# Moving columns read in runs of 16 from two halves of a row, and weight buffers on four places modulo 256 bytes

## The chip, the cores and the metric

The kernel runs on one core of a Trainium2 chip. The metric is the device time of one execution in microseconds (us). Before the change it is 827.43 us, the median of three runs (826.84 to 827.73).

The engines are named as the profile names them: PE (TensorE, matmuls), PEld (its weight loads, which run beside matmuls), DVE (VectorE), ACT (ScalarE), POOL (GpSimd) and SP (the queue that issues the transfers). SBUF is the working memory, 128 partitions wide; PSUM is where matmuls accumulate.

## The reference

A sigmoid attention is followed by a channel mix. All of it is float32; the inputs are scaled by factors that are left out here.

```python
# q, k, v: (8, 12, 448, 64)
scores = scale * np.matmul(q, k.transpose(0, 1, 3, 2)) - np.log(S)
attn = 1.0 / (1.0 + np.exp(-scores))
attn_out = np.matmul(attn, v)
x = attn_out.transpose(0, 2, 1, 3).reshape(B, S, H * D)       # (8, 448, 768)
x_prev = np.concatenate([np.zeros((B, 1, D)), x[:, :-1, :]], axis=1)
xk = mu_k * x + (1.0 - mu_k) * x_prev
xr = mu_r * x + (1.0 - mu_r) * x_prev
k = np.maximum(xk @ w_k, 0.0)                                 # 768 -> 1024
v = k * k @ w_v                                               # 1024 -> 768
r = 1.0 / (1.0 + np.exp(-(xr @ w_r)))                         # 768 -> 768
return r * v
```

## The kernel before, in words

The program has two parts, each planned by a small list scheduler (`Plan`): every operation has an engine, an assumed cost and a priority, and the planner writes the instructions in the order of the start times that it works out. The costs in it are numbers of the source, and the change doesn't touch them.

The first part is attention. Pairs of heads are worked on in quarters of the PE array: line 315 makes scores (`sc`), ACT takes the sigmoid into `pf`, line 327 multiplies by v into `av`, and DVE mixes neighbouring rows and sends xr and xk to DRAM. Beside this DVE converts the weights, which arrive as 64-bit floats, and forms the sums of weight quarters that the second part needs.

The second part is three stages of products: stage 0 is xr with w_r, stage 1 is xk with w_k, stage 2 is k squared with w_v. The 3584 tokens are cut into seven blocks of 512 (`TB`). The first block is done with four plain products (`SINGLE`); the other six go in three pairs, each with seven products instead of eight (the scheme of Strassen and Winograd, `ORDER = (0, 1, 4, 5, 6, 2, 3)`). One product `p` of a stage needs a weight matrix, its sum of quarters, and an operand, a sum of blocks of the input. Both are kept as two float32r tiles, a rounded part `hi` and the rest `lo`, and a product is three matmuls: weights hi by operand hi, hi by lo, lo by hi.

The weights of a product lie in one of seven buffers, `slots`, in the order of `ORDER`: product 0 in slot 0, 1 in slot 1, 4 in slot 2, 5 in slot 3, 6 in slot 4, 2 in slot 5, 3 in slot 6. The first half of a slot is hi, the second lo. A weight slice is 128 columns (512 bytes a partition). The operands lie in `rra` and `rrb`, in rows of 512 columns (2048 bytes). `multiply` issues the matmuls of one block of 128 outputs into a PSUM bank of 512 columns, `xb` or `yb`; `evacuate` reads the bank out on ACT and DVE. In stages 0 and 1 each block takes 9 matmuls, in stage 2 it takes 12; a product has 3, 4 and 3 blocks, so 27, 36 and 36 matmuls. With 25 products a stage this is 675, 900 and 900.

The pool `wp` holds the slots, then `rra`, `ysa` and the buffers of the conversion, counted up from the low end of SBUF. The pool `kp` of the second part ends at the high end and holds `rrb`, `ysb` and the buffers for evacuation; its last tile, `gap`, holds nothing and only shifts the others.

Of the kernel before, what the change touches and what calls it, by code (L numbers as in the profile page):

```python
# [8 lines left out]
F32 = mybir.dt.float32  # L9
F32R = mybir.dt.float32r  # L10
# [12 lines left out]
class Plan:  # L23
# [7 lines left out]
    def op(self, engine, cost, prio, run, reads, writes, dma=None):  # L31
        i = len(self.ops)
        deps = set()
        for r in reads:
            if r in self.writer:
                deps.add(self.writer[r])
        for w in writes:
            if w in self.writer:
                deps.add(self.writer[w])
            deps.update(self.readers.get(w, ()))  # L40
        for r in reads:
            self.readers.setdefault(r, []).append(i)
        for w in writes:
            self.writer[w] = i
            self.readers[w] = []
        deps.discard(i)
        self.ops.append(Op(engine, cost, prio, run, deps, dma))
# [51 lines left out]
def attention_then_channel_mix(  # L99
# [15 lines left out]
    nc = tc.nc  # L115
    P = 128
# [12 lines left out]
    WO = NJH * DF // 2  # L129
# [26 lines left out]
    def ring(pool, name, bufs, shape, dtype):  # L156
        return [pool.tile(shape, dtype, name=f"{name}{i}") for i in range(bufs)]

    wp = ctx.enter_context(tc.tile_pool(name="wp", bufs=1, side="left"))
    att = ExitStack()  # L160
    slots = [wp.tile([P, 2 * WO], F32R, name=f"slot{g}") for g in range(7)]
    RU = 2 * NJH
    rra = wp.tile([P, 2 * RU, TB], F32R, name="rra")
    ysa = wp.tile([P, RU, TB], F32, name="ysa")
# [18 lines left out]
    def mm(n, cols=S):  # L183
        return n * max(cols / 2.4 + 3.5, 205)
# [4 lines left out]
    def dve(n, fast=False, ptr=False):  # L189
        return 69 + n / (1.92 if fast else 0.96) + 61 * ptr  # L190
# [86 lines left out]
    def slot_of(stage, p):  # L277
        g = POS[p]
        n = TILES[stage] * WIDTH[stage]
        return slots[g][:, :n], slots[g][:, n:2 * n], ("slot", g)  # L280
# [175 lines left out]
    for t in range(T + LAG):  # L456
        n, j = t // NV * 2, t % NV
# [6 lines left out]
        n, j = (t - LAG) // NV * 2, (t - LAG) % NV  # L464
# [13 lines left out]
    kp = ctx.enter_context(tc.tile_pool(name="kp", bufs=1, side="right", reuse_waits="tile"))  # L478
# [3 lines left out]
    p1s = ring(kp, "p1s", 4, [P, TB], F32)  # L482
    u2 = ring(kp, "u2", 4, [P, TB], F32)
    cc = ring(kp, "cc", 5, [P, TB], F32)
    kp.tile([P, 48], F32, name="gap")
    pb = ctx.enter_context(tc.tile_pool(name="pb", bufs=1, space=PSUM, reuse_waits="tile"))
    yb = ring(pb, "yb", 4, [P, TB], F32)
    xb = ring(pb, "xb", 4, [P, TB], F32)
# [10 lines left out]
    def load_weight(stage, p, at):  # L499
        out7 = (None, wk_o, wv_o)[stage]  # L500
        hi, lo, K = slot_of(stage, p)
        for h in range(WO // TB):
# [4 lines left out]
            op(ACT, act(TB, True), at, lambda h_=h_, w=w: nc.scalar.copy(h_, w), [W], [K + (h, "hi")])  # L507
            op(DVE, dve(TB), at, lambda h_=h_, l_=l_, w=w: nc.vector.tensor_sub(l_, w, h_), [W, K + (h, "hi")], [K + (h, "lo")])  # L508

    def multiply(stage, s, p, i, at):  # L510
        xs = p in ((0, 1) if s < 0 else (0, 1, 4, 2))
        bank, K = (xb[i], ("xb", i)) if xs else (yb[i], ("yb", i))
        first = p in (0, 5, 4)
        hi, lo, R = used[stage, s, p]
        whi, wlo, W = slot_of(stage, p)
        n, w = TILES[stage], WIDTH[stage]

        def go():
            for t in range(n):
                c = slice(t * w + i * P, t * w + (i + 1) * P)  # L520
                for e, (a, b) in enumerate(((whi[:, c], hi[:, t]), (whi[:, c], lo[:, t]), (wlo[:, c], hi[:, t]))):
                    nc.tensor.matmul(bank, a, b, start=first and t == 0 and e == 0, stop=t == n - 1 and e == 2, skip_group_check=True)  # L522

        reads = R + [W + (h, a) for h in range(WO // TB) for a in ("hi", "lo")]
        op(PE, mm(3 * n, TB), at, go, reads, [K])
# [60 lines left out]
    for stage in range(3):  # L586
        for s in range(-1, NS):
            for p in SINGLE if s < 0 else ORDER:
                if (stage, s, p) not in used:
                    right(stage, s, p, at + PREP)  # L590
                for i in range(ROWS[stage]):
                    multiply(stage, s, p, i, at + i / ROWS[stage])
                    evacuate(stage, s, p, i, at + i / ROWS[stage] + EVAC)
                if stage < 2 and s == NS - 1:
                    load_weight(stage + 1, p, at + 1.2)
                at += 1
# [36 lines left out]
```

## Time and profile before

| | us |
|---|---|
| median of the runs | 827.43 |
| profiled execution, its own time | 826.25 |
| profiled execution, span of its instructions | 824.5 |
| PE busy | 816.1 |
| PEld busy | 649.6 |
| DVE busy | 616.4 |
| ACT busy | 428.8 |
| mean granted clock of PE | 0.999 |

The times of single instructions come from the profiled execution. Matmuls are pipelined, so a matmul's own duration is longer than the step from one matmul to the next; the step is read from the chain of work in order of time. The duration's end is modelled by the profiler. "Idle before" is the time that an engine stood still ahead of a group of instructions, with what ended it.

### The profile page before, as it was taken

The numbers are of one execution on the slowest core, as the hardware profiler recorded it, in microseconds if no ns is written. First come the engines' busy times: TensorE is split into PE (matmuls) and PEld (weight loads), VectorE is DVE, ScalarE is ACT, GpSimd is POOL, SyncE is SP. The second block draws the span as 40 slices with busy tenths as digits, with TensorE's granted clock in tenths as the row PEclk, the third lists the DMA queues.
The fourth block names the chain that finished last, engine by engine and source line by source line (L and its number), as shares of the span: only waits on it lengthen the run. The fifth ranks groups of instructions, "written<-read, shape, count | busy, mean of one in ns | idle before, by whom it ended". The sixth has DMA issues, their size and how long they took to land.

```text
span 824.5 us, 14185 instructions
## 1 busy us (share of the span) xinstructions
PE 816.1 (99%) x5163; PEld 649.6 (79%) x5163; DVE 616.4 (75%) x1060; ACT 428.8 (52%) x657; POOL 9.4 (1%) x100
## 2 busy tenths in 40 slices
PE   8999999999999999999999999999999999999997
PEld 5777777777777888888888888888888888888886
DVE  1978987878779889899995385394767749959854
ACT  5667776666663545455456466377574323323320
POOL 0000000000000000000000000000000000000000
PEclk9999999999999999999999999999999999999999
DMA  8778878899977693849783626434755366457304
GB/s 293 261 259 289 290 259 263 300 317 305 324 247 247 242 325 126 285 149 300 243 275 143 204 96 206 159 118 141 267 177 204 128 230 190 139 182 231 127 27 153
DMA packets 104405, 179.73 MB, mean 218 GB/s; under 512 B 13328, under 2 KB 59920, under 8 KB 102544
## 3 DMA queue, kind: packets, MB, share of 16 engines
q1 hardware_dynamic: 104336, 178.83, 64.8%
q8 instruction: 41, 0.67, 0.4%
q14 instruction: 28, 0.23, 0.1%
HBM read 109.06 MB, written 69.73 MB: 217 GB/s over the span
## 4 chain that ended last, share of the span: by engine, by line
PE 99%; DMA 0%; DVE 0%; issue 0%
PE xb L522 38%; PE yb L522 30%; PE sc L315 16%; PE av L327 15%; DMA raw<-in_qk 0%; DVE cc L577 0%; DVE cc L547 0%
## 5 line engine op out<-in xcount | busy, mean ns | idle before, releaser
L318 ACT ACTIVATE pf<-sc 128x896 f32<-128x896 f32 x168 | 154.0, 917 | 90.7 <-PE sc L315 90.3
L315 PE MATMUL sc<-raw 64*64 64x448 f32 x1344 | 187.9, 541 | 3.6 <-DMA raw<-in_qk 3.6
L327 PE MATMUL av<-pf,vn 64*64 64x448 f32 x1344 | 185.9, 536 | 0.0
L522 PE MATMUL xb<-rra,slot 128*128 128x512 f32 x717 | 173.9, 389 | 0.0
L522 PE MATMUL xb<-rrb,slot 128*128 128x512 f32 x669 | 162.2, 389 | 0.0
L522 PEld LDWEIGHTS xb<-rra,slot 128*128 128x128 f32 x717 | 134.5, 188 | 28.6 <-PE av L327 0.7
L522 PE MATMUL yb<-rra,slot 128*128 128x512 f32 x618 | 150.8, 389 | 0.0
L522 PEld LDWEIGHTS xb<-rrb,slot 128*128 128x128 f32 x669 | 125.6, 188 | 26.1
L522 PEld LDWEIGHTS yb<-rra,slot 128*128 128x128 f32 x618 | 116.0, 188 | 24.0
L315 PEld LDWEIGHTS sc<-raw 64*64 64x64 f32 x1344 | 92.4, 134 | 39.0 <-DMA raw<-in_qk 5.0
L327 PEld LDWEIGHTS av<-pf,vn 64*64 64x64 f32 x1344 | 92.5, 133 | 33.7 <-ACT pf L318 0.4
L522 PE MATMUL yb<-rrb,slot 128*128 128x512 f32 x471 | 116.3, 389 | 0.0
L522 PEld LDWEIGHTS yb<-rrb,slot 128*128 128x128 f32 x471 | 88.4, 188 | 18.3
L403 ACT CAST rra<-ysa 128x512 fp32r<-128x512 f32 x88 | 52.3, 619 | 49.6 <-PE yb L522 21.4
L404 DVE TENSOR_TENSOR rra<-ysa,rra 128x512 fp32r<-128x512 f32 x76 | 49.9, 686 | 11.1 <-ACT rra L403 10.9
L342 DVE TENSOR_SCALAR xo<-av,omr 128x447 f32<-128x447 f32 x48 | 32.5, 678 | 31.8 <-PE av L327 31.7
L403 ACT CAST rrb<-ysa 128x512 fp32r<-128x512 f32 x60 | 35.4, 616 | 39.1 <-PE yb L522 16.0
L404 DVE TENSOR_TENSOR rrb<-ysa,rrb 128x512 fp32r<-128x512 f32 x60 | 39.0, 685 | 10.4 <-ACT rrb L403 10.4
L563 DVE TENSOR_TENSOR u<-yb,p1s 128x512 f32<-128x512 f32 x30 | 20.7, 691 | 32.7 <-PE yb L522 32.4
L508 DVE TENSOR_TENSOR slot<-cc,slot 128x512 fp32r<-128x512 f32 x42 | 28.0, 686 | 18.7 <-ACT slot L507 18.6
L561 ACT COPY p1s<-xb 128x512 f32<-128x512 f32 x30 | 17.6, 588 | 37.9 <-PE xb L522 37.9
L541 ACT ACTIVATE cc<-cc 128x512 f32<-128x512 f32 x56 | 35.3, 631 | 1.0
(61 smaller groups left out, 656.8 us busy)
## 6 DMA issues: line engine op xcount, KB each, us to landing
k_d<-cc SPq DMA_DIRECT2D x56, 256.0 KB, 2.2
raw<-in_qk SPq DMA_DIRECT2D x48, 256.0 KB, 4.2
vn<-in_v SPq DMA_DIRECT2D x48, 224.0 KB, 5.0
xr_d<-xo SPq DMA_DIRECT2D x48, 224.0 KB, 3.9
xk_d<-xo SPq DMA_DIRECT2D x48, 224.0 KB, 3.9
r_d<-cc SPq DMA_DIRECT2D x42, 256.0 KB, 2.4
out<-cc SPq DMA_DIRECT2D x42, 256.0 KB, 3.3
raw<-in_qk SPq DMA_DIRECT2D x48, 192.0 KB, 4.5
```

The source lines that it names most:

```text
L315: nc.tensor.matmul(u[half[h ^ (m % 2)], m % 2, :S], x[half[h], c], x[half[h], D:D + S], start=True, stop=True)
L318: op(ACT, act(2 * S), at, lambda: nc.scalar.activation(f, u[:, :, :S], AF.Sigmoid, bias=NEG_LOG_S, scale=SCALE), [("sc", t % 2)], [("pf", ...
L327: nc.tensor.matmul(av[bank(m)][half[r ^ (m % 2)], :S], vn[m % RAW][half[r], j, :], pf[t % PFB][half[r], m % 2, :], start=j == 0, stop=j == ...
L342: op(DVE, dve(S, ptr=True), at, lambda y=y, om=om: nc.vector.tensor_scalar_mul(y[:, 1:], x[:, :S - 1], om[:, j:j + 1]), [X, ("om", key)], [Y])
L403: op(ACT, act(TB, True), at, lambda t=t: nc.scalar.copy(hi[:, t], y[:, t]), [Y[t]], [H[t]])
L404: op(DVE, dve(TB), at, lambda t=t: nc.vector.tensor_sub(lo[:, t], y[:, t], hi[:, t]), [Y[t], H[t]], [L[t]])
L508: op(DVE, dve(TB), at, lambda h_=h_, l_=l_, w=w: nc.vector.tensor_sub(l_, w, h_), [W, K + (h, "hi")], [K + (h, "lo")])
L522: nc.tensor.matmul(bank, a, b, start=first and t == 0 and e == 0, stop=t == n - 1 and e == 2, skip_group_check=True)
L541: op(ACT, act(TB, True), at, lambda: nc.scalar.activation(c, c, AF.Square), [C], [C])
L561: op(ACT, act(TB), at, lambda: nc.scalar.copy(p1s[i], x), [X], [P1])
L563: op(DVE, dve(TB), at, lambda: add(u2[i], y, p1s[i]), [Y, P1], [U2])
```

## The change

The matmuls of the three stages read their moving operand, and write their PSUM bank, in another order of columns. A row of 512 columns is seen as two halves (`h`) of 16 runs (`r`) of 16 columns (`c`, 64 bytes), and is gone through by run, then half, then column: columns 0 to 15, 256 to 271, 16 to 31, 272 to 287 and so on. The bank is addressed in the same order, so each result stands where it stood. Weight slices are read as before.

Tiles that hold nothing are put before and behind the slots, and each slot is made 16 words (64 bytes) longer, without use of them. Start addresses in the built program, modulo 256 bytes:

| tile | before | after |
|---|---|---|
| slot 0, 1, 2, 3, 4, 5, 6 | 32 each | 0, 64, 128, 192, 0, 64, 128 |
| rra, ysa, wraw, wbit, wexpo | 32 | 0 |
| rrb, ysb, p1s, u2, cc | 32 | 0 |

The tiles of the attention part (raw, vn, pf, xo) stay where they are, at 224. The instructions stand in the same order on every engine.

```diff
-    slots = [wp.tile([P, 2 * WO], F32R, name=f"slot{g}") for g in range(7)]
+    wp.tile([P, 56], F32, name="gap0")
+    slots = [wp.tile([P, 2 * WO + 16], F32R, name=f"slot{g}") for g in range(7)]
+    wp.tile([P, 16], F32, name="gap1")
...
-    kp.tile([P, 48], F32, name="gap")
+    kp.tile([P, 56], F32, name="gap2")
...
+    def zigzag(x):
+        return x.rearrange("p (h r c) -> p r h c", h=2, c=16)
+
...
-                    nc.tensor.matmul(bank, a, b, start=first and t == 0 and e == 0, stop=t == n - 1 and e == 2, skip_group_check=True)
+                    nc.tensor.matmul(zigzag(bank), a, zigzag(b), start=first and t == 0 and e == 0, stop=t == n - 1 and e == 2, skip_group_check=True)
```

## The prediction, made before the result was known

> **What bounds the kernel now.** I read the page first: the shares by engine, the granted clock, then the chain that ended last.
>
> ```profile
> span 824.5 us, 14185 instructions
> PE 816.1 (99%) x5163; PEld 649.6 (79%) x5163; DVE 616.4 (75%) x1060; ACT 428.8 (52%) x657; POOL 9.4 (1%) x100
> PEclk9999999999999999999999999999999999999999
> PE 99%; DMA 0%; DVE 0%; issue 0%
> PE xb L522 38%; PE yb L522 30%; PE sc L315 16%; PE av L327 15%; DMA raw<-in_qk 0%; DVE cc L577 0%; DVE cc L547 0%
> ```
>
> TensorE ends everything, at a full granted clock. 68% of the chain are the matmuls of line 522, the only ones that the change rewrites. Next the chain in order of time, to see how evenly that part runs:
>
> ```profile
> 8.88 0.75 PE sc L315 x8
> ...
> 49.48 0.75 PE sc L315 x8
> ...
> 326.00 18.36 PE xb L522 x81
> ...
> 558.56 24.48 PE xb L522 x108
> ...
> 811.52 8.17 PE yb L522 x36
> ```
>
> The columns are start, length, engine, tile, line, count. 18.36/81, 24.48/108 and 8.17/36 are all 226.7 to 226.9 ns a matmul, early and late, into xb and into yb. The groups by line give the counts, and the weight loads beside them:
>
> ```profile
> L522 PE MATMUL xb<-rra,slot 128*128 128x512 f32 x717 | 173.9, 389 | 0.0
> L522 PE MATMUL xb<-rrb,slot 128*128 128x512 f32 x669 | 162.2, 389 | 0.0
> L522 PE MATMUL yb<-rra,slot 128*128 128x512 f32 x618 | 150.8, 389 | 0.0
> L522 PE MATMUL yb<-rrb,slot 128*128 128x512 f32 x471 | 116.3, 389 | 0.0
> L522 PEld LDWEIGHTS xb<-rra,slot 128*128 128x128 f32 x717 | 134.5, 188 | 28.6 <-PE av L327 0.7
> L315 PE MATMUL sc<-raw 64*64 64x448 f32 x1344 | 187.9, 541 | 3.6 <-DMA raw<-in_qk 3.6
> L315 PEld LDWEIGHTS sc<-raw 64*64 64x64 f32 x1344 | 92.4, 134 | 39.0 <-DMA raw<-in_qk 5.0 <-ACT pf L318 1.1
> ```
>
> 717 + 669 + 618 + 471 = 2475 matmuls with no idle time before them: 2475 x 226.7 ns = 561.0 us, which is the stretch of the three stages. The rest of the 824.5 us is 258.4 of attention ahead and about 5 behind the last matmul, while the last block leaves; neither is rewritten. So the question is one number, the 226.7 ns.
>
> Is there air in it? In the attention part the chain goes from 8.88 to 49.48 us in 54 steps of eight records, 0.752 us each. An op there issues four products, one to each quarter of the array, and the trace has two records for each. If each record streams its 448 columns twice (my reading, not shown), a step is 4 x 448 columns and a column takes 0.420 ns. At that rate 512 columns take 214.9 ns, 11.8 ns less than 226.7. So the stages' matmuls lose at most about 11.8 ns each, and 2475 x 11.8 = 29.2 us is the most that any reordering of their reads can give back, if it can give anything. [...]
>
> **The change, part by part.** No instruction is added, removed or moved: on each engine the rows stand as before, and the planner's costs are untouched. Two things differ for the matmuls.
>
> *The places.* In the built program before, all seven slots, rra and rrb start at 32 modulo 256 bytes, and every weight slice and moving row is a multiple of 512 bytes further on. After, rra and rrb are at 0, and the slots at 0, 64, 128, 192, 0, 64, 128. By the products that use each slot (99 matmuls for one product over the three stages), 693 matmuls take weights at 0, 693 at 64, 792 at 128 and 297 at 192. The other tiles move by some bytes with them; their DVE and ACT rows are off the path, and I cost that at nothing, covered by the idle time below.
>
> *The order of the columns.* Each moving read, and each PSUM write with it, alternates between the halves of a row every 16 columns (64 bytes). No row shows a matmul with broken runs, so I bound it from both sides.
>
> The price of a broken run. The nearest rows are DVE's conversions:
>
> ```profile
> L213 DVE SCALAR_TENSOR_TENSOR wbit<-wraw,wbit 128x384 uint32<-128x384 uint32 (+1 forms) x40 | 23.8, 596 | 0.8
> L242 DVE TENSOR_TENSOR wbit<-wbit 128x384 f32<-128x384 f32 (+1 forms) x40 | 23.1, 595 | 0.6
> ```
>
> Line 213 reads every second word of wraw, line 242 reads two contiguous tiles; 596 against 595 ns. A stride costs that engine nothing, so the low end for TensorE is 0. For the high end I take one column's time for each of the 32 runs: 32 x 0.42 = 13.4 ns, x 2475 = +33 us. I take 0, by the row that is nearest. [...]
>
> The gain. My theory of the 11.8 ns is that a weight load, which runs beside the matmul ahead of it, and that matmul's moving read now and then want the same part of a partition's memory, and the moving read waits. The change has the form that fits four such parts of 64 bytes, repeating every 256. The load rows give the speeds: 188 ns for 128 columns and 134 for 64, so 54/64 = 0.84 ns a weight column, twice the 0.42 of a moving column. Read straight on, the moving stream goes through the parts twice as fast as the weights, so during a load of 128 x 0.84 = 108 ns it sweeps past the weights' part twice (8 parts against 4), whatever the starting places. Read in runs from both halves, which lie 1024 bytes apart and thus on the same part, it stays 32 columns, 13.4 ns, on each, exactly as long as the weights stay on theirs: 16 x 0.84. The two then go in step, and whether they meet depends on the slot's place alone.
>
> On a place where they never meet, the loss is 0. Where they meet, the moving read falls back until it has left the weights' part: between 0 and two parts' time, 26.9 ns. With four places a quarter of the cycle apart, two neighbours meet at least partly, and their losses together lie between one part's time (13.4) and three (40.3). Over four places this is 3.4 to 10.1 ns a matmul, against 11.8 now. The phase is not known from the trace; I take the middle, 6.7, and so a gain of 5.1 ns: 2475 x 5.1 = 12.6 us. The ends are 1.7 x 2475 = 4 and 8.4 x 2475 = 21 us. (The uneven use of the places, 297 to 792, shifts this within the same ends.)
>
> *Does the cover hold?* A faster TensorE can uncover VectorE. The stages by their stretches:
>
> ```profile
> core 0: us, PE busy (x) PEld busy (x) DVE busy (x) ACT busy (x) POOL busy (x), PEclk, DMA share, GB/s
> 258.30:421.00 162.70, 162.70 (x719) 134.72 (x718) 147.67 (x269) 78.99 (x141) 0.00 (x0) 1.00 0.73 246
> 421.00:620.00 199.00, 199.00 (x879) 164.83 (x879) 125.14 (x203) 122.06 (x217) 0.00 (x0) 1.00 0.51 171
> 620.00:819.50 199.50, 199.50 (x881) 165.05 (x880) 143.39 (x228) 60.81 (x101) 0.00 (x0) 1.00 0.50 163
> ```
>
> Stage 0 is the tight one: VectorE has 147.7 of 162.7 us, because the conversion of w_v runs there. 5.1 ns x 719 would shorten the stretch by 3.7 us, and VectorE has 15 idle. I keep the gain, and note that the full 11.8 ns (8.5 us) would leave it only 6.5 us of slack.
>
> The sum, against the profiled execution: 826.25 (824.5 of span and 1.75 around it) - 12.6 = 813.7. The median of the runs shown is 827.43, 1.2 us more, so I predict 815.
>
> **The rivals.** *Nothing happens.* The loss could be a fixed cost of a matmul that changes its weights, since a uniform 226.7 is just what a fixed cost looks like. For it: the evenness, over four pairs of tiles. Against: all those pairs have the same places, so an address cost would be as even; and the load is not the limit, since the first load group is idle 28.6 us for 134.5 busy. Time: 826 to 829. [...]
>
> *All of it goes.* Places that meet may lose next to nothing, if the moving read needs to give way only once. Then 2475 x 8.4 to 11.8 leaves 798 to 806 us. For it, the attention rate; against it, VectorE in stage 0.
>
> *Slower, by the runs.* Each broken run costs a column's time on the SBUF or the PSUM side: up to 827.4 + 33 = 860; half of that, 16 columns, eats the likeliest gain of 12.6 and gives 831. It decides from 5.1 ns a matmul, 12 columns' time in 32 runs. For it only that no matmul with runs is in the trace.
>
> [...]
>
> **How the numbers follow.** A measurement of this kernel tells about 0.2% (1.7 us) from no change. Partial gain, 806 to 825 us: 0.42, the highest since it follows from the speeds of the two streams, though the theory behind it is argued only. All of it, 798 to 806: 0.10. Nothing: 0.18. Slower by the runs: 0.14; slower by the places: 0.16. So faster 0.52, same 0.18, slower 0.30. The range: the lower end 802 leaves out half of the full gain (0.05); the upper end 843 leaves out the upper third of the runs' rival and the worst place, about 0.12. The likeliest case's own range is 806 to 825.
>
> **What would show it.** Right: the line of the stages' matmuls has steps that differ by slot, some near 215 ns (0.420 x 512), others longer, and the same for one slot in all stages; attention ends at 258.4 us as before; TensorE still holds 99% of the chain. Wrong: one even step again (226.7: nothing; over that: the runs' cost), or steps that change with the tile pair and not with the slot. A stage 0 that gains less than its share of matmuls, with TensorE idle behind VectorE's rows, would mean that the cover is gone. What would overturn the forecast most simply is a price for the broken PSUM runs.

## The result: 4% slower, one even step of 240.0 ns

The changed kernel takes 859.65 us (median; 859.44 to 860.05) against 827.13 us for the kernel before beside it: a ratio of 1.0394, 95% interval 1.038 to 1.0408. The prediction was 815, within 802 to 843. It was wrong in sign and in range.

The page of the changed kernel, in the parts that were shown of before:

```profile
span 857.7 us, 14186 instructions
PE 849.3 (99%) x5163; PEld 640.6 (75%) x5163; DVE 617.9 (72%) x1060; ACT 430.6 (50%) x657; POOL 9.3 (1%) x100
PEclk9999999999999999999999999999999999999999
PE xb L527 39%; PE yb L527 30%; PE sc L317 15%; PE av L329 15%; DMA raw<-in_qk 0%; DVE cc L582 0%; DVE cc L552 0%
```

TensorE still ends everything, at a granted clock of 1.000 (0.999 before), and VectorE and ScalarE are busy as long as before to within 2 us. The chain in order of time (start, length, engine, tile, line, count):

```profile
330.18 19.44 PE xb L527 x81
...
576.42 25.92 PE xb L527 x108
...
844.26 8.65 PE yb L527 x36
```

19.44/81 and 25.92/108 are 240.0 ns, early and late, in every stage and for both banks. In the group shown before, the weight loads grew from 188 to 191 ns and have more idle time before them (28.6 us before):

```profile
L527 PE MATMUL xb<-rra,slot 128*128 128x512 f32 x717 | 183.4, 403 | 0.0
L527 PEld LDWEIGHTS xb<-rra,slot 128*128 128x128 f32 x717 | 136.8, 191 | 35.8 <-PE av L329 0.7
```

Before, the step was 226.7. The difference of 13.3 ns, over 2475 matmuls, is 33.0 us; the two profiled executions differ by 859.44 - 826.25 = 33.2. Nothing else moved: the first matmul of the stages starts at 258.6 us, before at 258.4. By the start times in the trace the step is 240.0 on all seven slots, in all three stages.

### The profile page after: what moved, and what is told of

It reads as the page before. It is cut to its first block, busy times and chain, and to the rows that moved or that the text cites. A ratio compares the mean times of both kernels' runs of the same rounds, so it can differ in the third digit from the quotient of the medians.

```text
span 857.7 us, 14186 instructions
## 1 busy us (share of the span) xinstructions
PE 849.3 (99%) x5163; PEld 640.6 (75%) x5163; DVE 617.9 (72%) x1060; ACT 430.6 (50%) x657; POOL 9.3 (1%) x100
## 4 chain that ended last, share of the span: by engine, by line
PE 99%; DMA 0%; DVE 0%; issue 0%
PE xb L527 39%; PE yb L527 30%; PE sc L317 15%; PE av L329 15%; DMA raw<-in_qk 0%; DVE cc L582 0%; DVE cc L552 0%
## 5 line engine op out<-in xcount | busy, mean ns | idle before, releaser
L317 PE MATMUL sc<-raw 64*64 64x448 f32 x1344 | 199.1, 541 | 3.6 <-DMA raw<-in_qk 3.6
L329 PE MATMUL av<-pf,vn 64*64 64x448 f32 x1344 | 197.0, 536 | 0.0
L527 PE MATMUL xb<-rra,slot 128*128 128x512 f32 x717 | 183.4, 403 | 0.0
L527 PE MATMUL xb<-rrb,slot 128*128 128x512 f32 x669 | 171.1, 403 | 0.0
L527 PEld LDWEIGHTS xb<-rra,slot 128*128 128x128 f32 x717 | 136.8, 191 | 35.8 <-PE av L329 0.7
L527 PE MATMUL yb<-rra,slot 128*128 128x512 f32 x618 | 159.1, 403 | 0.0
L317 PEld LDWEIGHTS sc<-raw 64*64 64x64 f32 x1344 | 87.7, 134 | 47.7 <-DMA raw<-in_qk 5.2
L527 PE MATMUL yb<-rrb,slot 128*128 128x512 f32 x471 | 122.7, 403 | 0.0
L329 PEld LDWEIGHTS av<-pf,vn 64*64 64x64 f32 x1344 | 87.7, 133 | 42.4 <-ACT pf L320 0.4
L406 DVE TENSOR_TENSOR rrb<-ysb,rrb 128x512 fp32r<-128x512 f32 x36 | 22.9, 686 | 19.3 <-ACT rrb L405 19.3
```

What stands on the lines that cost most here:

```text
L317: nc.tensor.matmul(u[half[h ^ (m % 2)], m % 2, :S], x[half[h], c], x[half[h], D:D + S], start=True, stop=True)
L329: nc.tensor.matmul(av[bank(m)][half[r ^ (m % 2)], :S], vn[m % RAW][half[r], j, :], pf[t % PFB][half[r], m % 2, :], start=j == 0, stop=j == ...
L406: op(DVE, dve(TB), at, lambda t=t: nc.vector.tensor_sub(lo[:, t], y[:, t], hi[:, t]), [Y[t], H[t]], [L[t]])
L527: nc.tensor.matmul(zigzag(bank), a, zigzag(b), start=first and t == 0 and e == 0, stop=t == n - 1 and e == 2, skip_group_check=True)
```

## Experiments: which half of the change costs

Below, "the step" is the mean time from one matmul's start to the next in the trace, without the first of all, which is over 330 ns in every kernel (335 in the kernel before, 343 in the changed one). Diffs show the lines that matter. All kernels keep the order of instructions. A time without a ratio is that of one execution; the kernel before, beside it, took 826 to 828 us each time.

**Places alone, and runs alone.**

```diff
# e1, from the changed kernel
-nc.tensor.matmul(zigzag(bank), a, zigzag(b),
+nc.tensor.matmul(bank, a, b,
# e2, from the kernel before
-nc.tensor.matmul(bank, a, b,
+nc.tensor.matmul(zigzag(bank), a, zigzag(b),
```

> The changed kernel with its places and with the columns read and written straight on. If the broken runs alone cost the 13.3 ns that a step grew by (240.0 against 226.7), the step is 226.7 ns again on every slot and the time about 827 us. If the places cost it, the step is 240.0 and the time about 859. If a weight load and the moving read beside it meet on a part of a partition, as the prediction had it, the step differs between slots at 0, 64, 128 and 192.

> The kernel before with the runs of 16 and with its own places (all at 32 modulo 256). If the runs alone cost it: 240.0 ns a step, about 859 us. If the places do: 226.7 and 827. If a run that starts at 32 modulo 64 bytes costs more than one that starts at 0, more than 240.

Places alone: 837.35 us against 827.27, ratio 1.0124 (1.0107 to 1.014). The step differs by slot: 227.2 and 227.1 ns on the slots at 0, 233.2 and 233.3 at 64, 232.4 and 232.5 at 128, 229.1 at 192. Runs alone, on the old places: 860.61 us, 240.0 on every slot, so it does not matter either whether a run starts at 32 modulo 64 bytes, as here, or at 0, as in the changed kernel (240.0 too). Two readings of the chain, first e1, then e2, at the same products:

```profile
473.61 16.43 PE yb L527 x72
490.04 8.40 PE xb L527 x36
```

```profile
482.43 17.28 PE yb L525 x72
499.71 8.64 PE xb L525 x36
```

In e1 72 matmuls take 16.43 us (228 ns; slots at 192 and 0) and the 36 after them 8.40 (233; a slot at 64); in e2 17.28 and 8.64 are 240.0 both. So the runs cost the 33 us, the places cost 10 when the read is straight, and the two don't add: with runs the place no longer shows.

**Read side or PSUM side.**

```diff
# e3: read in runs          # e4: write in runs
-nc.tensor.matmul(zigzag(bank), a, zigzag(b),
+nc.tensor.matmul(bank, a, zigzag(b),
+nc.tensor.matmul(zigzag(bank), a, b,
```

> The changed kernel with the moving operand read in runs and the PSUM bank written straight on, so the columns of a block come out mixed. If a break costs a cycle on the PSUM side: 226.7 ns a step, 827 us. If on the SBUF side: 240.0 ns, 859 us. If each side costs a part, between them.

> The changed kernel with the moving operand read straight on and the PSUM bank written in runs, columns mixed. The mirror of the run before: 240.0 ns and 859 us if the PSUM side pays, 226.7 and 827 if the SBUF side does. If both stay at 226.7, the cost needs both together; if both are at 240, either one is enough and they overlap.

Read in runs: 859.47 us and 240.0 ns a step; the chain at the same products is that of e2:

```profile
481.40 17.28 PE yb L527 x72
498.68 8.64 PE xb L527 x36
```

Write in runs: 837.00 us, and over the whole stream, the first step included, a step takes 230.83 ns as in e1 (230.83), which writes straight. The same two lines of its chain are those of e1, 16.43 and 8.40 us:

```profile
473.37 16.43 PE yb L527 x72
489.80 8.40 PE xb L527 x36
```

Writing a PSUM bank in runs of 16 adds nothing to this stream (230.83 ns a step either way); the whole cost is in the moving operand's read from SBUF (240.0 in e3, where the bank is written straight).

## Experiments: why a read in runs costs

**Is it one column's time a run?** The 13.3 ns are close to 32 x 0.42 = 13.4, which tempts one to say so. (The expectations below take 0.417 ns a column, an estimate from 13.3 ns over 32 runs, where the prediction took 0.420; 512 columns are then 213.3 ns, and a straight step is 13.3 ns longer in place of 11.8.)

```diff
# e5, from the kernel before: runs of 32, 8, 64 columns in stages 0, 1, 2
+RUN = (32, 8, 64)
+    return x.rearrange("p (h r c) -> p r h c", h=2, c=c)
```

> The kernel before with its own places; the columns go by runs of 32 in stage 0, of 8 in stage 1 and of 64 in stage 2, again from two halves in turn. If each run costs one column's time more (0.417 ns, as 13.3 ns for 32 runs): steps of 233.3, 253.3 and 230.0 ns. If the cost belongs to any such pattern, whatever its runs: 240.0 in all stages. If it comes from runs being shorter than some block the read fetches (64 bytes, say), stages 0 and 2 stay at 226.7 and stage 1 pays more than 253.

Measured (848.46 us): 236.7, 243.3 and 226.7 ns, where one column's time a run asked for 233.3, 253.3 and 230.0. Two lines of the chain, for runs of 32 and of 8:

```profile
284.67 19.17 PE xb L527 x81
...
515.22 26.28 PE xb L527 x108
```

With 8, 16, 32 and 64 runs a row the extra is 0, 10.0, 13.3 and 16.7 ns. The fit at 32 runs was chance. Runs of 64 have an access pattern of as many dimensions as the others and cost nothing (226.7 ns), so the cost is not that of a longer pattern in the instruction.

**What are the 13.3 ns of the straight read, and does the weight load set either cost?**

```diff
# e6: COLS = (512, 480, 448, 384) by row tile; e10: COLS = (448, 480, 384) by stage
+nc.tensor.matmul(bank[:, :N], a, b[:, :N],
# e7: M = (128, 64, 64, 128) by row tile; e11: M = (64, 32, 96) by stage
+nc.tensor.matmul(bank[:m], a[:, :m], b,
# e10 and e11: straight, runs of 16, straight, runs of 8 by groups of token blocks
+RUN = (None, 16, None, 8)
```

> The kernel before with the matmuls of row tile t = 0, 1, 2, 3 cut to 512, 480, 448 and 384 moving columns; the part of the sums that this leaves out is missing in the output. It asks what the 13.3 ns are by which a straight step (226.7) exceeds 512 columns at 0.417. If one cycle is lost in each 16 columns read: 226.7, 212.5, 198.3, 170.0 ns, as far as weight loads keep up. If the loss is fixed for a matmul: 226.7, 213.3, 200.0, 173.3. If a weight load sets a floor, the shorter ones stop at it.

> The kernel before with 448, 480 and 384 moving columns in stages 0, 1, 2 (the rest of the sums left out), straight in token blocks 0, 3 and 4, by runs of 16 from two halves in blocks 1 and 2, by runs of 8 in 5 and 6. The halves lie 896, 960 and 768 bytes apart: 128, 192 and 0 modulo 256. If the same place twice running costs, the runs add nothing in stages 0 and 1 and 10 ns or more in stage 2. If each break costs a share, the runs add 28/32, 30/32 and 24/32 of 13.3 ns: 11.7, 12.5, 10.0. If the loss arises only while a weight load reads, it is 13.3 in all three. The straight blocks tell whether the 13.3 ns over the pure column time are fixed (200.0, 213.3, 173.3) or one cycle in 16 columns (198.3, 212.5, 170.0).

> The kernel before with weight slices of 64 columns in place of 128 for row tiles t = 1 and 2 (their other 64 outputs miss that part of the sum). If the 13.3 ns are lost to reads of weights (one cycle for each 16 bytes of them), the step beside a load of 64 columns is about 220 ns; if they belong to the moving read or are fixed, it stays at 226.7.

> The kernel before with weight slices of 64, 32 and 96 columns in stages 0, 1, 2 (the other outputs miss their sums), straight in token blocks 0, 3 and 4, by runs of 16 in blocks 1 and 2, by runs of 8 in 5 and 6. If the loss from runs arises where a weight load and the moving read meet, it shrinks with the load: about 7, 3 and 10 ns for runs of 16. If it is the moving read's own, it stays at 13.3 in all three. The same holds for the 13.3 ns of the straight order: 220, 217 and 223 ns if they belong to the load, 226.7 if not.

Columns: in e6 (800.60 us), where lengths alternate, the means are 234 (512), 217.4 (480), 207.8 (448) and 175.3 ns (384), longer than either rule. In e10 (780.40 us) TensorE waits for VectorE in places (7.3 us in all), so medians are given: straight 173 ns for 384 columns, which is the loss fixed for a matmul (173.3) and not one in proportion to the columns (170.0); 203 for 448 and 217 to 220 for 480 fit neither. From 384 to 512 columns the straight step grows by 53 to 54 ns, 0.42 a column, which agrees with the prediction's reading of the attention rows. Runs of 16 raise the medians to 180 (384), 213 (448) and 228 ns (480), runs of 8 to 185, 213 and 227. So a run pays also where the halves are 128 or 192 bytes apart modulo 256, and at all three lengths runs of 16 pay less than the 13.3 ns at 512 columns. The rule in columns stays open.

Weights: the loads of e11 (851.70 us) did get shorter,

```profile
L530 PEld LDWEIGHTS xb<-rra,slot 128*96 128x96 f32 x261 | 42.3, 162 | 19.0
...
L530 PEld LDWEIGHTS xb<-rrb,slot 128*32 128x32 f32 x240 | 26.3, 110 | 29.8
```

but not the steps. Its chain, where stage 1 (32 weight columns) goes by runs of 16 and then straight:

```profile
456.21 21.60 PE xb L530 x90
...
512.37 25.02 PE xb L530 x108
```

21.60/90 is 240.0 ns in runs and 25.02/108 is 231.7 straight. With 64 and 96 weight columns runs of 16 take 240.0 too, runs of 8 take 243.3 in all three stages, and the straight read 230 (e7, 831.39 us: 229.7 and 230.5 on the row tiles with 64). The straight read got 3 to 5 ns longer beside a shorter load. So neither cost shrank with the load (110 to 162 ns in e11, 188 before).

**Do the weights' places matter by themselves?** In e1 the operands had moved too. Here only the slots move.

```diff
# e8, from the kernel before: slots beyond the operands' place, in bytes modulo 256
+REL = (16, 32, 48, 96, 208, 224, 240)
```

> The kernel before, straight reads, with the seven slots 16, 32, 48, 96, 208, 224 and 240 bytes beyond the operands' place modulo 256. With the places 0, 64, 128, 192 the steps were 226.7, 233, 232 and 229 ns. If a weight load and a moving read meet on parts of 64 bytes, the steps rise smoothly between those values, and 226.7 is the lowest that there is. If 226.7 still holds conflicts, one of the new places is below it, down to 213.3, and a kernel with all slots there would be faster than both.

840.18 us. By slot: 231.6, 233.1, 233.2, 234.1, 231.9, 233.3 and 228.5 ns. The chain shows 72 matmuls on the slots 96 and 208 bytes beyond, 233.1 ns on average:

```profile
474.39 16.78 PE yb L529 x72
```

No place is below the common one of the kernel before. Since only the load reads a slot while TensorE works on it, a load does act on the matmul's step, by up to 7.4 ns, through where it reads. That is in keeping with the meeting that the prediction supposed, for the straight read, though no trace shows a meeting itself; but the best place is the same place (226.7 in the kernel before), and the steps do not rise smoothly between e1's four values (229.1 ns at 192 bytes, 231.9 at 208, 233.3 at 224, 228.5 at 240), as four parts of 64 bytes would have it.

**Other orders of the same runs.** "Halves", "quarters" and "eighths" are parts of a row from which a run is taken in turn. With "steps of 128 bytes" a row is gone through in several passes, each with one run from every 128 bytes; these steps are distances, not times. Stage 0 of e14 takes runs of 4 columns with steps of 128, 64 and 256 bytes.

```diff
# e9 and e14, from the kernel before: x is the moving row and the bank
+    if kind == "halves":
+        return x.rearrange("p (h r c) -> p r h c", h=h, c=c)
+    return x.rearrange("p (r h c) -> p h r c", h=h, c=c)      # kind == "step"
```

> The kernel before, its places, with another order of the columns in each group of products (reads and writes alike; the first token block straight). Stage 0, runs of 16: every second run, then the rest (step 128 bytes); every fourth run (step 256); four quarters in turn (step 512, four runs on one place). Stage 1: runs of 32 with steps of 256 and 512, runs of 64 with a step of 512. Stage 2: runs of 8 with steps of 64, 128, 256. If a break costs by itself, all orders with the same run length cost the same: about 240 for 16, 237 for 32, 243 for 8, 226.7 for 64. If the cost comes from the next run falling on the same place modulo 256 as the one before, the step of 128 is near 226.7 and the steps of 256 and the four quarters are far above 240, as are runs of 8 at 256. If only the halves' 1024 bytes matter, all stay at 226.7.

> The kernel before, its places, with nine more orders. [...] Stage 1: runs of 8 from four quarters and from eight eighths in turn, runs of 4 from two halves. Stage 2: runs of 16 from eight eighths, runs of 2 with steps of 128 bytes, runs of 4 from eight eighths. If alternating between two places 128 bytes apart is what made runs of 8 short, runs of 4 at 128 are near 220 too, and the orders that stay on one place modulo 256 (steps of 256, eighths of 256 bytes) are long. If shorter runs always cost more, runs of 4 are above 243 and runs of 2 above that.

| run, columns | order | step, ns |
|---|---|---|
| 64 | two halves / step 512 bytes | 226.7 / 226.8 |
| 32 | two halves / step 256 / step 512 | 236.7 / 236.6 / 233.4 |
| 16 | two halves / step 128 / step 256 | 240.0 / 240.0 / 239.5 |
| 16 | four quarters / eight eighths | 231.4 / 239.5 |
| 8 | two halves / four quarters / eight eighths | 243.3 / 231.1 / 258.2 |
| 8 | step 64 / step 128 / step 256 | 233.3 / 220.0 / 258.8 |
| 4 | step 64 / step 128 / step 256 | 226.6 / 246.6 / 278.0 |
| 4 | two halves / eight eighths | 250.1 / 278.1 |
| 2 | step 128 | 472.9 |

The values are from one execution each of e9 (844.82 us), e14 (934.29), e5 and e2. Neither run length nor the number of breaks orders this table. Staying on one place modulo 256 (256-byte steps, eighths) costs more than two halves only for runs of 8 (258.2 and 258.8 against 243.3) and 4 (278.1 and 278.0 against 250.1), and a step of 128 bytes, short for runs of 8 (220.0), is not short for runs of 4 (246.6). Runs of 2 columns (8 bytes) take 472.9 ns, about twice the straight 226.7. One broken order was shorter than the straight one, for 252 matmuls on end (e9: runs of 8 with steps of 64, then 128, then 256 bytes; then e14's runs of 2):

```profile
658.77 25.20 PE xb L535 x108
...
717.57 23.77 PE xb L535 x108
...
773.02 27.95 PE xb L535 x108
```

```profile
738.37 51.02 PE xb L535 x108
```

**Is the short order a faster kernel?** All matmuls in runs of 8 with steps of 128 bytes; then the same on the changed kernel's places.

```diff
# e12, from the kernel before
+nc.tensor.matmul(stride(bank), a, stride(b),     # "p (r h c) -> p h r c", h=4, c=8
# e13, from the changed kernel, by groups of token blocks
+FORM = ((None, ("step", 4, 8), ("step", 4, 8), ("halves", 4, 16)),) * 3
```

> The kernel before, its places, with the order that was shortest among the patterns, in all matmuls of the stages: runs of 8 columns (32 bytes) that step on by 128 bytes, four passes over a row. If the 220.0 ns a step that it showed in two thirds of a stage holds everywhere: 2475 x 6.67 = 16.5 us less than before, 810 us, a ratio of 0.980. If it depends on what surrounds it, or VectorE ends stage 0, between 810 and 827.

> The changed kernel's places (slots at 0, 64, 128, 192 beside operands at 0), the first token block straight, blocks 1 to 4 in runs of 8 with steps of 128 bytes, blocks 5 and 6 in runs of 16 from four quarters in turn. Straight reads cost 226.7, 233, 232 and 229 ns by slot there. If the cost of an order is the moving read's own, as the even 240.0 of runs of 16 suggests, 220 and 231 ns hold on every slot. If it comes from meeting the weight load, the step differs by slot.

No: e12 takes 837.19 us, ratio 1.0126 (1.0109 to 1.0143). The step is 230.7 ns throughout, on the same places and in the same order that held 220.0 in e9:

```profile
714.13 24.91 PE xb L525 x108
```

The single steps tell more than the mean. In e9 they go 219, 221, 219, 221; in e12 230, 230, 237, 227, 229 over and over. The kernel before, behind its first step of 335, goes 229, 234, 235, 225, 230, 236, 229, 232, 231 and only then stays at 226.7.

e13 (838.38 us) has both cycles in one order and on one place. Two lines of its chain in stage 2, both for the slots at 192 and then 0:

```profile
681.88 16.08 PE yb L535 x72
...
739.49 16.48 PE yb L535 x72
```

On the slot at 192 the steps go 231, 230, 219 over and over both times. On the slot at 0 behind it they go 219, 221 in the first line (220.2 ns) and 230, 230, 237, 227, 229 in the second (230.6). Over the three stages there are six such entries. In three of them the slots change behind a 219, and 219, 221 follows; in the other three they change behind a 230, and the long cycle follows. So the matmuls fall into a cycle of steps, and on this slot the point of the cycle ahead at which the slots change goes with the one that follows.

**Do the matmuls ahead decide it?**

```diff
# e15: straight in the first block of stage 0; e16: steps of 64 in the first block of each stage
+FORM = ((None, A, A, A), (A, A, A, A), (A, A, A, A))            # A = ("step", 4, 8)
+FORM = ((("step", 2, 8), A, A, A),) * 3
# e17: the changed kernel's order behind the short one
+FORM = ((("step", 2, 8), A, ("halves", 2, 16), ("halves", 2, 16)),) * 3
```

> Runs of 8 with steps of 128 bytes in all matmuls, as in the run that came to 230.7 ns a step, but the first token block of stage 0 (108 matmuls) straight. The same order held 220.0 ns in one kernel and 230.7 in another on the same places. If the pair of a matmul's read and the load beside it falls into a steady step that the matmuls before decide, the order is the same and the step 220.0 after this start, some 811 us; if the step belongs to something else that differed, it is 230.7 again and 837.

> The same with the first token block of every stage in runs of 8 with steps of 64 bytes (233.3 ns), the order that stood before the 220.0 in the kernel that showed it. If the state decides: 220.0 in the other six blocks of every stage, 826.7 - 2079 x 6.67 ns + 396 x 6.67 ns = 815.5 us. If not: 837.

> Blocks 1 and 2 of every stage in runs of 8 with steps of 128 bytes, blocks 3 to 6 in the changed kernel's runs of 16 from two halves. It asks whether the changed kernel's 240.0 is also one of several steady steps. If it is, this start may give another step; if 240.0 is the only one for that order, it is there from the first matmul or within a few.

Both starts missed: 836.18 us (ratio 1.0109, 1.0092 to 1.0125) and 837.04 (1.0094, 1.0058 to 1.013), and the step is 230.7 behind either start. In e16's profile the order with steps of 64 bytes did not show e9's even 233, 233, 234 but a longer cycle of 229 to 237, so the state ahead was not the same as in e9. e16's six executions took 837.79, 837.86, 836.93, 828.99, 837.16 and 831.18 us, a spread of 8.9 us at granted clocks of 0.998 to 0.999, where nine of the kernel before beside it lie within 1.3; a short cycle that some executions fall into would do that, but of these only the one at 837.79 was profiled. That the matmuls ahead pick the cycle rests on e13's six entries; e15 and e16 did not bring the short one about, and for the kernels on the places of before it is argued, not shown. No kernel with another order was faster than the kernel before.

The changed kernel's order showed no second mean. In e17 (851.08 us), behind 230.7, it is at 240.0 within two matmuls:

```profile
665.41 24.92 PE xb L533 x108
...
723.55 25.92 PE xb L533 x108
```

## Why the prediction was wrong, point by point

*The bound and the count* were right: TensorE ends everything, 2475 matmuls are rewritten, and their step alone sets the time.

*The step that failed* is the price of a broken run: "I take 0, by the row that is nearest." The nearest row was VectorE's, where a strided read took 596 ns and a contiguous one 595; TensorE's broken read cost 13.3 ns a matmul, the high end of the bounds (33 us). The term was taken from another engine's reads, and its 0 decided the sign. A 0 was right for the PSUM write (e4: 230.83 ns, as in e1) and wrong for the SBUF read (e3: 240.0). Its own sign of this case, one even step above 226.7, is what came. With the bound at 33 us and a most likely gain of 12.6, an unmeasured price should have held more than 0.14 of the chance.

*The gain by going in step* fell. It asked for steps that differ by slot; they are 240.0 on every slot, on the old places too, and with loads of 32 to 128 columns. What was right in it is narrower: weights' places do act on a straight read (227.1 to 233.3 ns in e1, 228.5 to 234.1 in e8). What was wrong: "whatever the starting places" (the straight read differs by up to 7.4 ns with them), and that 226.7 holds a cost which better places would shed; it is the lowest straight step of all places tried. That there was air in it was right in part: e9's 220.0 took out 6.7 of the supposed 11.8 ns, by another order and for 252 matmuls only.

*The rival "Slower by the runs"* named 860 and the time is 859.65. Its size was right for this run length, by luck: its rule, a column's time for each run, was not right (e5: 236.7, 243.3 and 226.7 ns, where it asked for 233.3, 253.3 and 230.0), and the PSUM side has no part in it (e4: 230.83 ns in runs and straight).

*The chance of 0.16 for "slower by the places"*, and the worst place that the range's upper end reckons with, rest on a penalty at places that meet which no run shows. The runs showed at most 7.4 ns a matmul from a place with the straight read (e8), and none in runs of 16 (240.0 on every slot).

*The rival "Nothing happens"* is out: with the same instructions the order alone takes the step from 226.7 to 240.0 ns (e2), and moving the weights alone lengthens it by up to 7.4 ns (e8).

*The cover* of VectorE in stage 0 was not put to the test, since TensorE got slower (240.0 ns a step).

*Open:* why a read in these runs settles at 240.0, whether and where in memory the straight read and the load meet, and whether the short cycle of runs of 8 can be brought about at will.

## What to carry to other kernels

When a matmul stream is the bound, price a new access pattern with a row of TensorE itself, not of another engine (here 13.3 ns a matmul against VectorE's 1 ns in 596); a kernel with a different pattern in each stage gives several prices in one profile. Read the step between matmuls (18.36 us for 81, so 226.7 ns) rather than their durations (389 ns), and look at single steps: here an order that alternated between 219 and 221 ns in one kernel (e9) went by 230, 230, 237, 227, 229 in another (e12). For straight reads keep weights and moving operands on the same place modulo 256 bytes, the best of the places tried here (226.7 and 227.2 ns, against 228.5 to 234.1 on the others), until a run says otherwise, and don't trust one short stretch of a pattern for the whole kernel.

## What the runs showed that was not expected

- Runs of 16 columns in the moving read of a float32r matmul add 13.3 ns to 226.7; the same runs in the PSUM write add 0 (230.83 against 230.83 ns).
- Moving only the weight buffers, by 16 to 240 bytes modulo 256, lengthens the step from 226.7 to between 228.5 and 234.1 ns.
- One order on the same places held 220.0 ns in one kernel and 230.7 in four others, each for hundreds of matmuls; in e13 it held both on the same slot.
- With weight loads of 32 columns (110 ns) in place of 128 (188) the step is no shorter: 231.7 ns straight, against 226.7, and 240.0 in runs of 16, as with 128.
- Runs of 2 columns (8 bytes) take 472.9 ns a matmul.
